# A fixed order, read from a table, for the vector, scalar and transfer work beside a matmul-bound token phase

## The chip, the cores and the metric

The kernel runs on one core of a Trainium2 chip. The core has TensorE (PE, matmuls; the profile lists its weight loads apart as PEld), VectorE (DVE), ScalarE (ACT), GpSimd (POOL) and SyncE (SP, which here only issues transfers). Each engine works through its own queue in order; semaphores tie the queues together. The metric is the device time of one execution in microseconds.

## The reference

The input x is (8, 3008, 256). Every sequence is Fourier-transformed along its 3008 rows, mixed by a complex 256x256 weight, shrunk towards zero by 0.01, and transformed back. The 24064 resulting rows ("tokens") go through a two-layer network with a squared relu.

```python
X = np.fft.rfft(x, axis=1)
Yr = Xr @ w_r - Xi @ w_i + b_r
Yi = Xr @ w_i + Xi @ w_r + b_i
Yr = np.sign(Yr) * np.maximum(np.abs(Yr) - lam, 0.0)      # Yi likewise
y = np.fft.irfft(Yr + 1j * Yi, n=3008, axis=1)
h = y.reshape(24064, 256) @ w_in                          # 256 -> 2048
r = np.maximum(h, 0.0)
out = (s * (r * r) + b) @ w_out                           # 2048 -> 256
```

## The kernel before

3008 = 94 x 32, and each transform is done by matmuls in steps: one over the 94 (`s1_units`, matmuls `x,A_t` into `u`), a pass through DRAM that regroups rows (`ud`, loaded as `us`), one over the 32 with the mixing and shrinking (`s23_units`: `fwd_unit` makes `xf`, `sum_unit` makes `s`, `mix_unit` and `shrink` work in the tile `ring`, `inv_unit` makes `v`), another pass through DRAM (`vd`, loaded as `vs`), and the last transform (`s4_units`) into `yt`, the token activations in 16 bits, transposed. `shrink` ends with the row swaps: 64-partition pieces of `ring` are moved to other partitions by transfers that SP issues (line 732), four for each of a sequence's first ten units. Sequence 1 shrinks unit by unit; the later ones take two units at once, and then issue eight transfers.

The first sequence is done alone, in the first 47 us (`first_batch`). After that comes the token phase: 48 tiles of up to 512 tokens. A tile takes 16 slots (`mc`). In each slot the first layer's matmuls for 128 of the 2048 hidden columns go to the double bank `psh`; every second slot ends with a relu of 1024 columns from `psh` to the f32 tile `rt` (line 879, on ACT) and a square into the 16-bit tile `gt` (line 889 on ACT or line 892 on DVE). In between run the previous tile's second layer, from `gt` and `w_out_t` into the banks `psa`, and pieces of the next sequence's transforms, through the two banks `psf`. Which piece goes into which slot is written in `plan`.

Some tiles use a scheme with seven products in place of eight for the second layer (`seven_mms`). It needs sums of blocks of `gt` (`s_op`, line 990 on DVE, tiles `s` and `gt`, and one accumulating transfer on POOL, line 983) and prepared sums of w_out (`T_s`). Its results leave PSUM through DVE adds at line 1023 into `zz` and `ost`. Where only the two `psa` banks serve, the fourth product (`psa<-T_s,s`) needs the bank that products one and two filled, so it waits for two adds: one into `zz`, one into `ost`. The results are stored from `ost` by SP (line 907 for most tiles).

The order of the engines' queues is set by the framework's scheduler, which works from its own estimates and from priorities; copies out of PSUM, relus and final adds are marked urgent (`urgent()`). Whether a copy or a square goes to DVE or ACT is decided when the code is recorded, by running sums of estimated work (`evac`, `act_first`, `work`); relus always go to ACT and final adds to DVE.

Of the kernel before, what the change touches and what calls it, by code (L numbers as in the profile page):

```python
# [9 lines left out]
F16 = mybir.dt.float16  # L10
# [9 lines left out]
VSCALE = 1.0 / 64.0  # L20

# [75 lines left out]
def kernel(  # L97
# [70 lines left out]
    lean = [0.0]  # L168

    pe = {"on": False, "now": 0.0}  # L170

    def matmul(out, lhs, rhs, **how):
        if pe["on"]:
            pe["now"] += 0.0025 + int(np.prod(rhs.shape[1:])) / 2400.0
        return nc.tensor.matmul(out, lhs, rhs, **how)  # L175

    def work(engine, us):
        load[engine] = max(load[engine], pe["now"]) + us

    def act_first(ready, ta, td):  # L180
        return max(load["act"], ready) + ta <= max(load["dve"], ready) + td + lean[0]

    def urgent():

        return tc.high_priority(offset=200) if pe["on"] else nullcontext()

    def evac(dst, src, cols):
        ta, td = over["act"] + cols / 1200.0, over["dve"] + cols / 960.0
        with urgent():
            if act_first(pe["now"], ta, td):  # L190
                work("act", ta)
                return None, nc.scalar.copy(out=dst, in_=src)  # L192
            work("dve", td)
            return nc.vector.tensor_copy(out=dst, in_=src), None
# [3 lines left out]
    def mix_bank():  # L198
        return pools["m"].tile([P, 512], F32, name="psm", tag="psm")
# [10 lines left out]
    def two_banks():  # L210
        return pools["h"].tile([P, 2, 512], F32, name="psh", tag="psh")

    def one_bank():
        return fpool.tile([P, 512], F32, name="psf", tag="psf")
# [4 lines left out]
    def other_bank():  # L219
        return apool.tile([P, 512], F32, name="psa", tag="psa")  # L220
# [6 lines left out]
    def emit_load_x(b, first=None, chunks=range(N2 // XCH)):  # L227
        xv = x[b].rearrange("(n1 n2) d -> n1 (n2 d)", n2=N2)
        for c in chunks:
# [4 lines left out]
            if first is not None:  # L234
                gate = nc.gpsimd.tensor_copy(out=t[0:1, 0:1], in_=first)
# [133 lines left out]
    last_square = [None]  # L369
# [4 lines left out]
    def make_t(i):  # L374

        if not T_s:
            nc.vector.tensor_tensor(
                out=b_21, in0=bias_bc[:, P:D], in1=bias_bc[:, 0:P], op=ALU.subtract
            )
            T_s.append(x2pool.tile([P, 4, MC // 2, P], F16, name="T_s", tag="x2"))  # L380
        t = T_s[0]
        a, b, op = (
            (w_block(0, 1), w_block(0, 0), ALU.subtract),
            (t[:, 0], w_block(1, 1), ALU.subtract),
            (w_block(1, 1), w_block(0, 1), ALU.subtract),
            (w_block(1, 0), t[:, 1], ALU.add),
        )[i]
        with tc.issue_after(last_square[0].ins):
            nc.vector.tensor_tensor(out=t[:, i], in0=a, in1=b, op=op)
        work("dve", 0.61)  # L390
# [9 lines left out]
    def make_bias():  # L400
# [3 lines left out]
        nc.scalar.activation(out=bias_bc, in_=ps[:, 0:D], func=AF.Copy, scale=bb_bc)  # L404
# [3 lines left out]
    ring = []  # L408
    yts = {}
    tails = {}  # L410
# [3 lines left out]
    def first_batch():  # L414
# [121 lines left out]

        def turn(ec, n):

            ps = mix_bank() if ec == 0 else any_bank() if n < HW else one_bank()
            for j in range(4):  # L540
# [5 lines left out]
            evac(  # L546
                vs[(0, h)][:, k : k + 4, ec * P : (ec + 1) * P],
# [5 lines left out]
        def last_dft(ec, n):  # L553
# [5 lines left out]
            else:  # L559
                ps = other_bank() if n % 8 else one_bank()  # L560
            for j in range(4):
# [6 lines left out]
            evac(  # L568
                yt[:, ec, n : n + 4, :],
                ps[:, 0:384].rearrange("p (j n) -> p j n", n=96), 384,  # L570
            )

# [51 lines left out]
    def s1_units(b, more_banks=False):  # L624

        ud = dpool.tile([96, N2, D], F16, name="ud", tag="ud")
        hold = {}

        def unit(i):
# [4 lines left out]
            ps = any_bank() if more_banks else one_bank()  # L634
            matmul(
# [4 lines left out]
            evac(u[0:96, k : k + 2, :], ps[0:96, :].rearrange("p (j d) -> p j d", j=2), 512)  # L640
            if k == UCH - 2:
                n = 2 * i + 2
                nc.sync.dma_start(out=ud[:, n - UCH : n, :], in_=u[0:96])

        def take_rows(which=range(4)):
            uv = ud.rearrange("k n d -> (k n) d").rearrange("(q p) d -> p q d", p=P)
            for q in which:
                t = uspool.tile([P, 6, D], F16, name="us", tag="us")
                nc.sync.dma_start(out=t, in_=uv[:, 6 * q : 6 * q + 6, :])
                us[(b, q)] = t  # L650
# [3 lines left out]
    def s23_units(b):  # L654
# [6 lines left out]
        hold = {}  # L661

        def fwd_unit(i):
# [3 lines left out]
            t = us[(b, i // 3)]  # L667
            for j in range(2):
# [7 lines left out]
            evac(xt[:, 1:3].rearrange("p r c k -> p (r c k)"), bank, 512)  # L676
            nc.vector.tensor_tensor(out=xt[:, 0], in0=xt[:, 1], in1=xt[:, 2], op=ALU.add)  # L677
            work("dve", 0.34)
            xf[i] = xt

        def sum_unit(h):

            ps = one_bank().rearrange("p (i e) -> p i e", i=2)
# [6 lines left out]
            s = mpool.tile([P, 2, D], F32, name="s", tag="m")  # L690
            with urgent():
                nc.scalar.copy(out=s, in_=ps)
            work("act", 0.49)
            hold[h] = s

        def mix_unit(i):
            ps = one_bank().rearrange("p (r e) -> p r e", r=2)
            xt = xf.pop(i)
            for r in range(2):
# [5 lines left out]
            with urgent():  # L705
                nc.vector.tensor_tensor(  # L706
                    out=ring[0][:, i % 4], in0=ps,
                    in1=hold[i // 2][:, i % 2].unsqueeze(1).to_broadcast([P, 2, D]), op=ALU.add,
                )
            work("dve", 0.67)  # L710
# [5 lines left out]
        def shrink(i, n):  # L716
# [4 lines left out]
            nc.vector.tensor_tensor(out=m, in0=t, in1=lo, op=ALU.max)  # L721
            nc.vector.tensor_tensor(out=m, in0=m, in1=hi, op=ALU.min)
            nc.vector.tensor_tensor(out=t, in0=t, in1=m, op=ALU.subtract)
            work("dve", 0.21 + 0.8 * n)
            for k in range(i, i + n):
                z = ring[0][:, 6 + k % 6]
                for j in range(2):
                    for r in range(2):
                        o = z[64 * r : 64 * r + 64, j]
                        a = t[64 * j : 64 * j + 64, k - i, r]  # L730
                        if k < H - 2:
                            nc.sync.dma_start(out=o, in_=a)
                        else:
                            nc.vector.tensor_copy(out=o, in_=a)
                            work("dve", 0.13)
                zt[k] = z

        def inv_unit(i):
            ps = one_bank().rearrange("p (j e) -> p j e", j=2)
            z = zt.pop(i)  # L740
            for j in range(2):
# [7 lines left out]
            evac(v[:, h : h + 2, :], ps, 512)  # L749
            if i % 2 == 1:  # L750
                nc.sync.dma_start(
                    out=vd[2 * i - 2 : 2 * i + 2].rearrange("q p e -> p q e"), in_=v
                )
            if i == H - 1:
                hold["vv"] = vd.rearrange("q (k n) e -> (q k) (n e)", n=N2)
# [4 lines left out]
        def take_half(h):  # L760
            t = vspool.tile([96, HW, D], F16, name="vs", tag="vs")
            nc.sync.dma_start(
                out=t.rearrange("k n e -> k (n e)"),
                in_=hold["vv"][:, h * HW * D : (h + 1) * HW * D],
            )
            vs[(b, h)] = t
# [17 lines left out]
    def s4_units(b):  # L784
# [6 lines left out]
        def unit(g):  # L791
# [4 lines left out]
            ps = one_bank()  # L796
            for j in range(w):
# [6 lines left out]
            evac(  # L804
                yt[:, ec, n2 : n2 + w, 0:N1],
                ps[:, 0 : w * N1].rearrange("p (j n) -> p j n", n=N1), w * N1,
            )
            if g == len(groups) - 1 and b >= 2:
# [3 lines left out]
                nc.gpsimd.tensor_copy(out=tails[pr][:, :, half], in_=yt[:, :, :, 80:94])  # L812
# [22 lines left out]
    hold_h = {}  # L835

# [21 lines left out]
    def first_mm(ti, mc):  # L858
# [4 lines left out]
        ps = hold_h["ps"]  # L863
        for dc in range(DC):
# [12 lines left out]
        rt = rpool.tile([P, 2, 512], F32, name="rt", tag="rt")  # L877
        with urgent():
            nc.scalar.activation(out=rt[:, :, 0:w], in_=ps[:, :, 0:w], func=AF.Relu)  # L879
# [4 lines left out]
        rr = rt[:, :, 0:w]  # L884
        if halves(ti):
            rr = rr.rearrange("p k (i t) -> p k i t", i=2)
        work("act", 0.07 + w / 600.0)
        if act_first(pe["now"], 0.09 + w / 600.0, 0.07 + w / 480.0):
            nc.scalar.activation(out=gt, in_=rr, func=AF.Square)  # L889
            work("act", 0.09 + w / 600.0)  # L890
        else:
            last_square[0] = nc.vector.tensor_tensor(out=gt, in0=rr, in1=rr, op=ALU.mult)  # L892
            work("dve", 0.07 + w / 480.0)
    def store(tl, sub, src):
        kind, b, j, w = tl
        if kind == "wide":
# [3 lines left out]
            nc.sync.dma_start(  # L900
                out=rows[n2 : n2 + 4, lo : lo + w], in_=src[0 : 4 * w]
            )
            return
        if kind == "main":
            rows = out[b * N + 512 * j : b * N + 512 * (j + 1), :]
            rows = rows.rearrange("(n1 n2) d -> n2 n1 d", n2=N2)[8 * sub : 8 * sub + 8]
            nc.sync.dma_start(out=rows, in_=src)
# [4 lines left out]
        while i < end:  # L912
# [14 lines left out]
            nc.sync.dma_start(out=dst, in_=src[i - i0 : i - i0 + cnt])  # L927
            i += cnt

    def second_mms(ti):  # L930
# [6 lines left out]
        def mm(sub, mc):  # L937
# [3 lines left out]
            if h == 0 and mc == 0:  # L941
                hold["ps"] = sum_bank(ti).rearrange("p (h e) -> p h e", h=2)
            ps = hold["ps"]
            matmul(
# [5 lines left out]
            if mc == MC - 1 and (alone or h == 1 or sub == nsub - 1):  # L950
                k = h + 1
                ost = opool.tile([P, 2, D], F32, name="ost", tag="ost")
                with urgent():
                    nc.vector.scalar_tensor_tensor(  # L954
                        out=ost[0:size, 0:k], in0=ps[0:size, 0:k], scalar=s_bc[0:size],
# [3 lines left out]
                work("dve", 0.13 + 0.27 * k)  # L959
                for i in range(k):  # L960
                    store(tl, sub - k + 1 + i, ost[:, i, :])
# [7 lines left out]
    sums = {}  # L969

# [4 lines left out]
    def s_op(ti, n, q):  # L975

        size = 2 * sub_size(tiles[ti])
        if n == 1:
# [213 lines left out]
```

## Time and profile before

| | |
|---|---|
| median of 3 runs | 836.48 us (836.18 to 836.76) |
| profiled execution | 837.46 us, its span 835.7 us |
| TensorE clock granted | 1.00 |
| busy: PE / DVE / ACT / POOL | 820.7 / 703.9 / 723.0 / 86.3 us |
| chain that ended last | PE 78%, DVE 9%, ACT 5%, DMA 5% |
| relu, 128x1024 on ACT (line 879) | 327 in the token phase, 1.03 us each |
| square, 128x1024 on DVE / ACT | 207 of 1.22 us / 121 of 1.06 us |
| `ring<-ring` transfers of 32 KB | 280 |

The duration of an instruction on DVE or ACT includes its end phase, beside which the next one already starts; two squares on DVE that wait for nothing start 1.14 us apart. The chain names, for each moment, the work that the end of the execution depended on. A wait row reads: engine and line that waited, what released it, total us, times, longest us.

### The profile page before, as it was taken

To read this page: it belongs to the slowest core of one execution; us is meant where nothing else is said; L and a number is where in the kernel's file an instruction comes from. 1 tells how busy PE (TensorE), PEld (TensorE's weight loads), DVE (VectorE), ACT (ScalarE), POOL (GpSimd) and SP (SyncE) were. 2 spreads that over 40 slices of the span, in tenths; PEclk is the share of its full clock that TensorE was granted. 3 is DMA by queue.
4 is the path that set the end of the run, shared out by engine and by line. 5 is a ranking of instruction groups with operands and counts; after the bars stand their busy time and mean duration, and the time that the engine had idled before them with its cause. 6 is when DMAs were issued, how large, how long until landed. Compare 5 with 4: busy or idle time off the path is not lost.

```text
span 835.7 us, 19552 instructions
## 1 busy us (share of the span) xinstructions
PE 820.7 (98%) x7662; PEld 598.5 (72%) x7662; DVE 703.9 (84%) x1104; ACT 723.0 (87%) x962; POOL 86.3 (10%) x114
## 2 busy tenths in 40 slices
PE   7999999999999999999999999999999999999997
PEld 6857767777677767777677776777767777767765
DVE  5988979978898888987889888797888988879785
ACT  5998988998899988998899988989879988788882
POOL 4550001100011001100011000100001000001000
PEclk9999999999999999999999999999999999999999
DMA  8954578346773378445773458724565233513321
GB/s 201 178 155 102 116 193 208 61 97 138 193 185 66 96 182 200 124 104 137 182 191 71 97 137 208 183 48 114 128 178 141 59 103 100 135 45 77 77 62 59
DMA packets 116670, 107.17 MB, mean 128 GB/s; under 512 B 12774, under 2 KB 100842, under 8 KB 115234
## 3 DMA queue, kind: packets, MB, share of 16 engines
q1 hardware_dynamic: 102498, 80.55, 34.0%
q0 software_dynamic: 14080, 25.37, 19.1%
q8 instruction: 60, 0.98, 0.5%
q14 instruction: 32, 0.26, 0.1%
HBM read 53.52 MB, written 46.66 MB: 120 GB/s over the span
## 4 chain that ended last, share of the span: by engine, by line
PE 78%; DVE 9%; ACT 5%; DMA 5%; issue 2%; POOL 0%; SPq 0%; DVEq 0%; POOLq 0%
PE psh L175 32%; PE psa L175 28%; PE psf L175 17%; ACT rt L879 2%; DVE gt L892 2%; DMA vd<-v 1%; DMA ring<-ring 1%; DMA x<-in_x_dram 1%; DVE ring L706 1%; DVE gt L990 1%; PE psm L175 1%; DVE ost L1023 1%; DMA vs<-vd 1%; ACT gt L889 1%; DVE s L990 1%
## 5 line engine op out<-in xcount | busy, mean ns | idle before, releaser
L879 ACT ACTIVATE rt<-psh 128x1024 f32<-128x1024 f32 (+2 forms) x384 | 386.9, 1009 | 56.0 <-PE psh L175 54.0
L175 PEld LDWEIGHTS <-gt 128*128 128x128 f16 (+1 forms) x3696 | 304.9, 101 | 167.2 <-issue 0.5
L175 PE MATMUL psh<-yt,w_in 128*128 128x512 f16 (+1 forms) x1344 | 396.7, 378 | 0.1
L892 DVE TENSOR_TENSOR gt<-rt 128x1024 f16<-128x1024 f32 (+2 forms) x239 | 286.0, 1201 | 81.3 <-ACT rt L879 80.6
L175 PE MATMUL psa<-w_out_t,gt 128*128 128x256 f16 (+3 forms) x2448 | 310.3, 253 | 0.0
L175 PEld LDWEIGHTS <-w_in 128*128 128x128 f16 x1536 | 136.5, 98 | 25.4 <-issue 2.9
L889 ACT ACTIVATE gt<-rt 128x1024 f16<-128x1024 f32 (+2 forms) x145 | 150.8, 1040 | 3.4
L175 PE MATMUL psa<-T_s,gt 128*128 128x128 f16 (+1 forms) x944 | 79.4, 219 | 0.0
L983 POOL DMA_DIRECT2D gt<-gt x42 | 38.0, 905 | 325.7 <-PE psh L175 87.3
L192 ACT CAST u<-psf 96x512 f16<-96x512 f32 x96 | 55.7, 582 | 9.1 <-PE psf L175 8.4
L706 DVE TENSOR_TENSOR ring<-psf,s 128x512 f16<-128x512 f32 x84 | 57.4, 684 | 4.1 <-PE psf L175 3.1
L192 ACT CAST v<-psf 128x512 f16<-128x512 f32 x79 | 45.8, 583 | 14.0 <-PE psf L175 13.5
L175 PE MATMUL psh<-tail,w_in 128*128 128x512 f16 (+1 forms) x192 | 52.1, 352 | 0.0
L239 POOL DMA_DIRECT2D x<-in_x_dram x36 | 19.2, 538 | 315.6 <-PE psf L175 314.4
L175 PEld LDWEIGHTS <-xf 128*128 128x128 f16 x504 | 46.7, 98 | 5.8 <-DVE xf L677 0.4
L175 PE MATMUL psf<-W_g,xf 128*128 128x256 f16 x336 | 50.4, 272 | 0.0
L192 ACT CAST yt<-psf 128x470 f16<-128x470 f32 (+2 forms) x84 | 43.1, 535 | 3.4 <-PE psf L175 2.2
L1023 DVE SCALAR_TENSOR_TENSOR ost<-psa,s_bc,zz 128x256 f32<-128x256 f32 (+1 forms) x80 | 34.7, 477 | 7.9 <-PE psa L175 6.4
L954 DVE SCALAR_TENSOR_TENSOR ost<-psa,s_bc,bias_bc 128x512 f32<-128x512 f32 (+2 forms) x51 | 37.1, 727 | 4.8 <-PE psa L175 2.6
L192 ACT CAST xf<-psf 128x512 f16<-128x512 f32 x64 | 37.5, 586 | 3.8 <-PE psf L175 3.7
L175 PE MATMUL psf<-x,A_t 94*96 94x512 f16 x102 | 39.0, 382 | 1.0 <-ACT yt L192 0.3
L175 PE MATMUL psf<-C_t,vs 96*128 96x94 f16 (+1 forms) x484 | 38.0, 205 | 0.1
(118 smaller groups left out, 797.0 us busy)
## 6 DMA issues: line engine op xcount, KB each, us to landing
out_dram<-ost SPq DMA_DIRECT2D x152, 128.0 KB
ud<-u SPq DMA_DIRECT2D x56, 192.0 KB
us<-ud SPq DMA_DIRECT2D x28, 384.0 KB
vd<-v SPq DMA_DIRECT2D x42, 256.0 KB
vs<-vd SPq DMA_DIRECT2D x14, 768.0 KB
x<-in_x_dram POOLq DMA_DIRECT2D x28, 376.0 KB, 6.3
gt<-gt POOLq DMA_DIRECT2D x38, 256.0 KB, 4.2
ring<-ring SPq DMA_DIRECT2D x280, 32.0 KB
```

The lines of the kernel that those rows point to most:

```text
L175: return nc.tensor.matmul(out, lhs, rhs, **how)
L192: return None, nc.scalar.copy(out=dst, in_=src)
L239: nc.gpsimd.dma_start(out=t[0:N1, i * w : (i + 1) * w], in_=xv[:, c * XCH * D + i * w : c * XCH * D + (i + 1) * w],)
L706: nc.vector.tensor_tensor(out=ring[0][:, i % 4], in0=ps, in1=hold[i // 2][:, i % 2].unsqueeze(1).to_broadcast([P, 2, D]), op=ALU.add,)
L879: nc.scalar.activation(out=rt[:, :, 0:w], in_=ps[:, :, 0:w], func=AF.Relu)
L889: nc.scalar.activation(out=gt, in_=rr, func=AF.Square)
L892: last_square[0] = nc.vector.tensor_tensor(out=gt, in0=rr, in1=rr, op=ALU.mult)
L954: nc.vector.scalar_tensor_tensor(out=ost[0:size, 0:k], in0=ps[0:size, 0:k], scalar=s_bc[0:size], in1=bias_bc[0:size].unsqueeze(1).to_broad ...
L983: nc.gpsimd.dma_start(out=a12, in_=a11, accum_op=ALU.add)
L990: nc.vector.tensor_tensor(out=out, in0=a, in1=b, op=op)
L1023: nc.vector.scalar_tensor_tensor(out=out, in0=of, scalar=s_bc[0:size], in1=other, op0=ALU.mult, op1=ALU.add)
```

## The change

All work of the token phase on ACT, DVE, SP and POOL is recorded as pieces (`later`), each with what it needs and the engines that could do it. A table `TURNS` holds two characters in base 36 for each piece; their number gives the piece's engine (remainder by 4: act, dve, sp, pool) and how many pieces later than its place of recording it is emitted. `pump`, called at each matmul, emits the pieces whose turn has come, and the framework is told to keep the order in which things are emitted (`manual_schedule`, all five engines). So engine and order of 2,525 pieces are fixed by the table, relus may also go to DVE, and the running sums decide only in the first batch.

In `shrink` the swaps of two units are one transfer of 64 partitions x 2 x 256 in place of two: four transfers instead of eight for a pair. `rt` and `ost` become three fixed buffers each. The loads of x lose two of three gate copies, and the fourth chunk of a sequence's x is recorded at slot 44 or 48 of the sequence instead of 54. PE's order is the same but for the first tiles of the token phase, where first-layer matmuls stand before some `x,A_t` matmuls, and a few exchanged neighbours.

```diff
+TURNS = (
+    "25253y20241x21251w26241s24242e1p2h3m363m2q1d20181c1k1x1o1h20213g1g1x251w30232j231s1g1s1t3o1s"
...
     def matmul(out, lhs, rhs, **how):
-        if pe["on"]:
-            pe["now"] += 0.0025 + int(np.prod(rhs.shape[1:])) / 2400.0
+        pump()
         return nc.tensor.matmul(out, lhs, rhs, **how)
...
+    def plan_turns():
+        at = [divmod(int(TURNS[k : k + 2], 36), 4) for k in range(0, len(TURNS), 2)]
+        queue.extend(
+            (k, ("act", "dve", "sp", "pool")[at[k][1]])
+            for k in sorted(range(len(at)), key=lambda k: k + at[k][0])
+        )
+
+    def begin(op, engine):
+        assert engine in op.cost and all(n.gone for n in op.needs)
+        op.gone = True
+        op.emit(engine)
+
+    def pump():
+        while queue and queue[0][0] < len(pieces):
+            k, engine = queue.pop(0)
+            begin(pieces[k], engine)
...
+    def later(emit, cost, needs=(), frees=None):
+
+        op = SimpleNamespace(emit=emit, cost=cost, needs=list(needs), gone=False)
+        if frees is not None:
+            reads[id(frees)].append(op)
+        if pe["on"]:
+            pieces.append(op)
+            return op
...
+    def leave_bank(dst, bank, src, cols, needs=()):
+        def emit(e):
+            (nc.scalar.copy if e == "act" else nc.vector.tensor_copy)(out=dst, in_=src)
+
+        return later(emit, copy_cost(cols), needs=needs, frees=bank)
...
+            moves = []
+            for j in range(2):
+                for r in range(2):
+                    o = ring[0][64 * r : 64 * r + 64, z0 : z0 + n, j]
+                    a = t[64 * j : 64 * j + 64, :, r]
+                    if i + n <= H - 2:
+                        moves.append(later(
+                            lambda e, o=o, a=a: nc.sync.dma_start(out=o, in_=a),
+                            {"sp": 0.6 + 0.05 * n}, needs=[done],
+                        ))
+                        continue
...
-                        if k < H - 2:
-                            nc.sync.dma_start(out=o, in_=a)
-                        else:
-                            nc.vector.tensor_copy(out=o, in_=a)
-                            work("dve", 0.13)
...
+        def relu(e):
+            if e == "act":
+                nc.scalar.activation(out=rt, in_=ps[:, :, 0:w], func=AF.Relu)
+            else:
+                nc.vector.tensor_scalar(
+                    out=rt, in0=ps[:, :, 0:w], scalar1=0.0, scalar2=None, op0=ALU.max
+                )
...
+        first = later(
+            relu, {"act": 0.065 + w / 600.0, "dve": 0.065 + w / 480.0},
+            needs=squares[-len(rts) :][:1] if len(squares) >= len(rts) else [], frees=ps,
+        )
+        squares.append(later(
+            square, {"act": 0.1 + w / 600.0, "dve": 0.065 + w / 480.0}, needs=[first]
+        ))
...
-            nc.sync.dma_start(out=rows, in_=src)
+            send(rows.rearrange("(n1 n2) d -> n2 n1 d", n2=N2)[8 * sub : 8 * sub + 8], src)
...
+                a = add(base, 0, 0.39, needs=left_ops[-3:])
+                b = add(top, 1, 0.39, needs=[a, *new_o(0)])
...
+    plan_turns()
+    osts = [opool.tile([P, 2, D], F32, name="ost", tag="ost") for _ in range(3)]
+    rts = [rpool.tile([P, 2, 512], F32, name="rt", tag="rt") for _ in range(3)]
+    ctx.enter_context(tc.manual_schedule(engines={
+        mybir.EngineType.PE, mybir.EngineType.Activation, mybir.EngineType.DVE,
+        mybir.EngineType.SP, mybir.EngineType.Pool,
+    }))
...
-            for c, at in enumerate((10, 14, 26, 54)):
+            free_at = 37 + 4 * (mark[b] - s1 - 50) // 16
+            for c, at in enumerate((10, 14, 26, free_at)):
```

## The prediction

> **What bounds the kernel now.** I read the page first: the busy line, then the chain that ended last.
>
> ```profile
> PE 820.7 (98%) x7662; PEld 598.5 (72%) x7662; DVE 703.9 (84%) x1104; ACT 723.0 (87%) x962; POOL 86.3 (10%) x114
> ...
> PE 78%; DVE 9%; ACT 5%; DMA 5%; issue 2%; POOL 0%; SPq 0%; DVEq 0%; POOLq 0%
> ```
>
> TensorE (PE) sets the time; DVE and ACT are nearly full beside it and own 14% of the chain. A busy PE row hides small waits, because the end of a matmul is modelled: in the timeline a 128-column matmul is shown as 0.22 us, yet seven in a row start 0.055 us apart. So I took PE's spacing from start to start, against the median spacing of its shape (0.056 us for 128 columns, 0.109 for 256, 0.216 for 512). All matmuls at those medians make 806.6 us. What lies above them is 9.8 us before 46 us (the first batch, which the change leaves alone) and 13.7 us after. The latter is all that an order of the other engines can win. It splits into: 5.0 us in 9 places where `psa<-T_s,s` waits; 2.6 us in 16 places where a matmul into `psf` waits for a copy or sum of DVE or ACT; 1.7 us in 6 places at transfers (1.0 of it one wait at 111.8 us); 0.8 us in 4 places at the start of the token phase; 0.5 us at `psh` and at the end; and 3.1 us in pieces below 0.06 us, which I leave where they are.
>
> Next the waits. The largest is one pattern:
>
> ```profile
> PEld L175 <- DVE ost L1023: 5.1, 9, 0.9
> ...
> PE psf L175 <- DMA ring<-ring: 0.9, 1, 0.9
> ```
>
> The timeline of DVE at one of the nine, and PE's row that it released:
>
> ```profile
> 456.75 0.68 DVE L706 TENSOR_TENSOR ring<-psf,s 128x512 f16<-128x512 f32 x1
> 457.35 1.22 DVE L892 TENSOR_TENSOR gt<-rt 128x1024 f16<-128x1024 f32 x1
> 458.49 0.68 DVE L721 TENSOR_TENSOR ring<-ring,low 128x1024 f16<-128x1024 f16 x1
> 459.09 0.68 DVE L990 TENSOR_TENSOR gt<-gt 128x1024 f16<-128x1024 f16 x1
> 459.69 0.48 DVE L1023 SCALAR_TENSOR_TENSOR zz<-psa,s_bc,bias_bc 128x256 f32<-128x256 f32 x1
> 460.08 0.68 DVE L722 TENSOR_TENSOR ring<-ring,high 128x1024 f16<-128x1024 f16 x1
> 460.68 0.48 DVE L1023 SCALAR_TENSOR_TENSOR ost<-psa,s_bc,zz 128x256 f32<-128x256 f32 x1
> ...
> 460.07 0.50 PE L175 MATMUL psa<-T_s,gt 128*128 128x128 f16 x6
> 461.22 0.23 PE L175 MATMUL psa<-T_s,s 128*128 128x128 f16 x1 [0.65 <-DVE ost L1023]
> ```
>
> The two adds at L1023 empty the `psa` bank that PE wants. The last of the six matmuls starts at 460.07 + 5 x 0.0555; the next was due at 460.40 and came 0.81 us late. DVE never paused: a square (1.14), a `ring` step (0.60) and a `gt` sum (0.60) stand ahead of the adds, another `ring` step (0.60) between them. That is a matter of order. Last, the end:
>
> ```profile
> 829.65 0.48 DVE L954 SCALAR_TENSOR_TENSOR ost<-psa,s_bc,bias_bc 128x256 f32<-128x256 f32 x1 [0.56 <-PE psa L175]
> 831.40 0.48 DVE L954 SCALAR_TENSOR_TENSOR ost<-psf,s_bc,bias_bc 128x256 f32<-128x256 f32 x1 [1.26 <-PE psf L175]
> ...
> 829.12 3.40 SPq L907 DMA_DIRECT2D out_dram<-ost  x4
> ```
>
> SP sends three stores while PE still works; one store is left behind the last add, and the span ends 3.8 us after that add.
>
> **The change part by part.** The sum is made against the profiled execution: 837.46 us, of which the span is 835.7; the median of the runs is 0.98 below it.
>
> *Order on DVE around the adds.* Seventeen tiles before the last batch use this scheme with only two `psa` banks. As built, 13 of them had one DVE instruction between the two adds, now none has. At the place above, DVE now does the `ring` sum and three 16-bit sums (4 x 0.60) and then the two adds; the square has gone to ACT. From the same 456.75 the adds end at 456.75 + 2.40 + 0.39 + 0.48 = 460.02, before 460.40. The other seventeen places leave 0.9 to 1.6 us by the same kind of sum. Of 5.0 us I take 4.7 as gone. What is late next is the 3.1 us of small pieces. Bounds: nothing gone (0) to 5.0.
>
> *Copies, relus and squares dealt out anew.* Counts as built: on DVE 62 relus more (none before), 104 squares fewer, 116 copies out of PSUM more; ACT the reverse. Intervals from start to start when nothing waits: square 1.138 DVE, 0.965 ACT; copy of 512 columns 0.60 DVE, 0.48 ACT; relu 0.93 ACT. A relu on DVE isn't in the trace: between 1.138 (the square, as many f32 elements) and 1.20 (two copies); I take 1.14, one instruction being nearest to the square. DVE: 62 x 1.14 - 104 x 1.138 + 116 x 0.60 = +22 us; ACT: -58 + 100 - 56 = -14 us. Beside PE's 807 us both stay under 90%, so the work itself is hidden. If the cover failed everywhere, it would cost those 22 us on the path. [...]
>
> Does the new order serve PE's other waits? For each result of DVE or ACT that PE waits for after 60 us I set the intervals queued on its engine against PE's own spacing from release to need: 14 come out late in the old order, 2 (by 0.05 and less) in the new, and the rest have 0.3 us or more. Waits of DVE on ACT or transfers aren't in that sum, and it misses most of the 0.81 above, so I take 2.0 of the 2.6 us, not all. Bounds: -1 (new waits for a blocked queue) to 2.6.
>
> *Row swaps.* 280 transfers of 32 KB become 40 of 32 KB and 120 of 64 KB; 120 issues fewer. Eight issues take 5.6 us in the timeline of SP, so SP saves some 78 us; PE sees that only where a swap comes too late. The first of a pair is complete after four issues as before (2.8 us), the second 2.8 us sooner; each transfer carries twice the bytes. A swap lands 1.3 us after its issue by median, 6.5 at worst; a 256 KB `vd` write, the larger neighbour, 3.1. So 0 to 1.8 us more; I take little over 0. [...]
>
> But the fixed order on SP puts stores into the swaps of the second sequence (b = 1, not merged): the last swap of unit 9 now stands behind two stores. From there to PE's need I count 4.0 us less DVE's own lag of about 1, formerly 6.8. Landings at 100 to 110 us have a median of 4.8 and a worst of 6.3, so I expect 1.8 us of wait there and 0.5 elsewhere early (at 68 and 72 us of PE time 3.6 to 3.9 are left): 2.5 us of transfer waits in place of 1.7, a loss of 0.8. Bounds: a gain of 1.2 to a loss of 3.3.
>
> *POOL* issues one gate copy instead of three and asks for the fourth chunk of x some 6 to 10 slots earlier. It waited 314 us for PE before those loads; without that cover, a chunk takes 6.3 us to land and is wanted over 25 us later. Nothing.
>
> *Start of the token phase.* PE's order now has w_in matmuls where `x,A_t` matmuls stood. The first needs a copy of `yt` which DVE, backlogged there, delivers 2.5 us late by the queue's sum; the worst was 2.1. Loss 0.4; bounds 0 to 1.5.
>
> *The end.* As built, SP holds two earlier stores until after the last one. Issue spacing 0.65 us: the span's end moves by 2 x 0.65 = 1.3 us. Nothing hides that. Bounds 0.6 to 1.3.
>
> Sum: -4.7 - 2.0 + 0.8 + 0.4 + 1.3 = -4.2 us. 837.46 - 4.2 = 833.3 for a profiled execution, 836.48 - 4.2 = **832.3** for the median.
>
> **The rivals.**
> Nearly clean: swaps land in time and all 16 `psf` waits go too: -5.0 - 2.6 - 1.2 + 0.4 + 1.3 = -7.1, so 829.4, or 828 with a start that costs nothing and half of the small pieces. For it: the margins of the queue sums; against: landings of up to 6.5 us.
>
> No gain: DVE, 22 us fuller, reaches the adds as late as before, because what it waits for (ACT's relus: 80.6 us of waiting before L892) now blocks it in a fixed order. The 4.7 stay: 837.0. Against it: all seventeen places have the square moved away or margin.
>
> Slower: the fixed queue of SP as the new limit. Every sequence ends its swaps close ahead of PE's need; a swap behind a store that waits for DVE delays all seven. One us at each makes 832.3 + 7 = 839. It decides from 0.6 us each. For it: SP waited 78.9 us for L1023 adds at L907, with up to 13.1 in one piece. Against: 120 issues fewer, and margins of 5 us and more after b = 1.
>
> **How the numbers follow.** A run of this kernel tells from no change about 0.2%, 1.7 us: faster is below 834.8, slower above 838.2. Chances: the forecast 0.60 (its own range 830.3 to 834.7), nearly clean 0.18, no gain 0.11, slower 0.11. Range 828 to 837: it leaves out the slower case and little below. Faster 0.78, same 0.11, slower 0.11.
>
> **What would show it.** Waits of PE's weight loads for L1023's successor under 1 us in all, and the two adds side by side in DVE's timeline; relus on DVE of 1.14 us spacing; three stores on SP after the last add and 5 us from that add to the span's end; a `ring` wait near 110 us. The forecast is wrong if PE waits in new places behind SP or behind a DVE that stands still for ACT.

## The result and the profile after

The change made the kernel slower: 845.54 us (844.55 to 846.66, four runs) against 836.62 us (836.18 to 837.41), a ratio of 1.0106 with an interval of 1.0088 to 1.0123. I had forecast 832.3 us and a range that ends at 837. The profiled execution took 845.85 us, its span 844.1 us; before, the span was 835.7.

The page of the changed kernel, its busy line and its chain:

```profile
PE 821.6 (97%) x7662; PEld 601.3 (71%) x7662; DVE 729.1 (86%) x1178; ACT 705.8 (84%) x888; POOL 84.5 (10%) x112
...
PE 77%; DMA 11%; DVE 7%; ACT 3%; issue 1%; SPq 1%; POOL 0%; DVEq 0%; ACTq 0%; POOLq 0%
```

The share of DVE in the chain fell from 9% to 7%, that of the transfers rose from 5% to 11%: the end of the execution now depends on transfers for some 50 us more than before. PE's waits (and DVE's, where it waits for a transfer) say which transfers:

```profile
DVE ring L891 <- DMA ring<-ring: 4.6, 4, 2.6
...
PEld L235 <- DMA gt<-gt: 2.9, 3, 1.1
PE psf L235 <- DMA ring<-ring: 2.7, 4, 1.2
PEld L235 <- DMA vs<-vd: 2.6, 3, 1.5
PE psa L235 <- DMA gt<-gt: 2.4, 3, 0.9
PE psf L235 <- DMA vs<-vd: 2.1, 3, 1.3
PE psf L235 <- DVE xf L298: 1.5, 1, 1.5
PEld L235 <- DMA us<-ud: 1.0, 1, 1.0
```

A weight load and the matmul behind it often wait for the same transfer (`vs` above, 2.6 and 2.1 us in three waits each), so such rows aren't added. Every kind of transfer is there: swaps, both passes through DRAM (`us<-ud`, `vs<-vd`) and the accumulating `gt` transfers. The row that was the largest before, PE's weight loads behind the `ost` adds with 5.1 us, is gone. At the place that the prediction used, DVE and PE now show:

```profile
464.93 0.68 DVE L1268 TENSOR_TENSOR gt<-gt 128x1024 f16<-128x1024 f16 x1
465.53 0.68 DVE L1268 TENSOR_TENSOR s<-gt 128x1024 f16<-128x1024 f16 x1
466.25 0.69 DVE L1268 TENSOR_TENSOR gt<-gt 128x1024 f16<-128x1024 f16 x1
466.86 0.48 DVE L1325 SCALAR_TENSOR_TENSOR zz<-psa,s_bc,bias_bc 128x256 f32<-128x256 f32 x1
467.37 0.48 DVE L1325 SCALAR_TENSOR_TENSOR ost<-psa,s_bc,zz 128x256 f32<-128x256 f32 x1
...
468.33 0.44 PE L235 MATMUL psa<-T_s,gt 128*128 128x128 f16 x5
468.61 0.22 PE L235 MATMUL psa<-T_s,s 128*128 128x128 f16 x1
```

The two adds stand side by side behind three sums, as counted, and `psa<-T_s,s` follows 468.33 + 5 x 0.0555 without a wait. The end of the execution:

```profile
836.39 0.48 DVE L1225 SCALAR_TENSOR_TENSOR ost<-psa,s_bc,bias_bc 128x256 f32<-128x256 f32 x1 [1.00 <-PE psa L235]
838.14 0.48 DVE L1225 SCALAR_TENSOR_TENSOR ost<-psf,s_bc,bias_bc 128x256 f32<-128x256 f32 x1 [1.26 <-PE psf L235]
...
835.42 5.14 SPq L1162 DMA_DIRECT2D out_dram<-ost  x4
```

From the end of the last add (838.62) to the end of the span there are now 5.5 us, 3.8 before.

Measured as in the prediction (PE's spacing from start to start above the median of its shape), the 8.4 us of span come from these places, in us, each rounded by itself:

| | forecast | measured | before -> after |
|---|---|---|---|
| `psa<-T_s,s` behind the adds | -4.7 | -4.9 | 5.0 -> 0.1 |
| `psf` behind copies and sums | -2.0 | +1.3 | 2.6 -> 3.9 |
| transfers | +0.8 | **+9.2** | 1.7 in 6 places -> 10.9 in 14 |
| start of the token phase | +0.4 | +1.1 | 0.8 -> 1.9 |
| last matmul to the end of the span | +1.3 | +1.7 | 4.6 -> 6.3 |
| first batch, before 46 us | 0 | +0.8 | 9.8 -> 10.6 |
| all else, pieces below 0.06 us among it | 0 | -0.6 | |

One row carries the result. It is mostly not the speed of the transfers. From the traces I took, for each transfer, its landing time (end of the issue to landing) and its lead (end of the issue to the first matmul that reads it, with any wait of that matmul inside):

| us | landing, median: before | after | lead, smallest / median: before | after |
|---|---|---|---|---|
| `ring<-ring` | 1.3 | 1.8 | 3.8 / 9.2 | 1.9 / 7.3 |
| `vs<-vd` | 7.2 | 6.2 | 7.3 / 10.2 | 5.5 / 8.5 |
| `us<-ud` | 5.0 | 4.5 | 4.2 / 22.4 | 5.3 / 15.8 |
| `gt<-gt` | 3.5 | 3.9 | 3.8 / 7.4 | 4.1 / 6.2 |

By median, swaps and `gt` transfers land half a us later and the two passes half a us to one us sooner. The leads fell by 1.2 to 6.6 us by median, and for swaps and `vs` in the smallest too. PE waits where a lead would be shorter than the landing. Two things can make an issue late: what stands ahead of it on SP, and data that DVE finishes later. Both had changed. From the end of the second unit's mix to the end of the subtraction, a shrink of two units on DVE took 3.2 us before and 4.1 after, by median; and writes to `vd` whose data is ready stood on SP for 2.8 us in the median and 10.4 at most, 0.03 and 6.5 before.

### The profile page after: what moved, and what is told of

Its sections match the earlier page's. It is cut to its first block, busy times and chain, and to the rows that moved or that the text cites. A ratio compares the mean times of both kernels' runs of the same rounds, so it can differ in the third digit from the quotient of the medians.

```text
span 844.1 us, 19222 instructions
## 1 busy us (share of the span) xinstructions
PE 821.6 (97%) x7662; PEld 601.3 (71%) x7662; DVE 729.1 (86%) x1178; ACT 705.8 (84%) x888; POOL 84.5 (10%) x112
## 4 chain that ended last, share of the span: by engine, by line
PE 77%; DMA 11%; DVE 7%; ACT 3%; issue 1%; SPq 1%; POOL 0%; DVEq 0%; ACTq 0%; POOLq 0%
PE psh L235 31%; PE psa L235 28%; PE psf L235 16%; DMA ring<-ring 3%; DMA vs<-vd 3%; DMA gt<-gt 2%; DMA vd<-v 2%; PE psm L235 1%; DVE gt L1138 1%; ACT rt L1125 1%; ACT gt L1136 1%; DVE ring L891 1%; DMA x<-in_x_dram 1%; DVE rt L1127 1%; DMA us<-ud 1%
## 5 line engine op out<-in xcount | busy, mean ns | idle before, releaser
L1125 ACT ACTIVATE rt<-psh 128x1024 f32<-128x1024 f32 (+2 forms) x322 | 323.8, 1007 | 72.7 <-PE psh L235 67.6
L1136 ACT ACTIVATE gt<-rt 128x1024 f16<-128x1024 f32 (+2 forms) x249 | 256.0, 1042 | 6.6 <-DVE rt L1127 4.5
L1138 DVE TENSOR_TENSOR gt<-rt 128x1024 f16<-128x1024 f32 (+2 forms) x135 | 161.2, 1202 | 5.7 <-ACT rt L1125 5.1
L1127 DVE TENSOR_SCALAR rt<-psh 128x1024 f32<-128x1024 f32 (+1 forms) x62 | 74.1, 1197 | 21.3 <-PE psh L235 14.9
L891 DVE TENSOR_TENSOR ring<-psf,s 128x512 f16<-128x512 f32 x84 | 57.6, 686 | 21.4 <-PE psf L235 15.8
L298 DVE CAST u<-psf 96x512 f16<-96x512 f32 x53 | 36.0, 680 | 8.7 <-PE psf L235 8.5
L298 ACT CAST xf<-psf 128x512 f16<-128x512 f32 x59 | 34.1, 583 | 8.9 <-PE psf L235 8.8
L298 ACT CAST yt<-psf 128x470 f16<-128x470 f32 (+2 forms) x70 | 35.7, 519 | 4.2 <-PE psf L235 2.9
L298 ACT CAST v<-psf 128x512 f16<-128x512 f32 x43 | 25.0, 583 | 14.2 <-PE psf L235 14.2
```

The lines of the kernel that those rows point to most:

```text
L298: (nc.scalar.copy if e == "act" else nc.vector.tensor_copy)(out=dst, in_=src)
L891: lambda e: nc.vector.tensor_tensor(out=ring[0][:, i % 4], in0=ps, in1=hold[i // 2][:, i % 2].unsqueeze(1).to_broadcast([P, 2, D]), op=ALU ...
L1125: nc.scalar.activation(out=rt, in_=ps[:, :, 0:w], func=AF.Relu)
L1127: nc.vector.tensor_scalar(out=rt, in0=ps[:, :, 0:w], scalar1=0.0, scalar2=None, op0=ALU.max)
```

## The experiments

Theories at the start: A, transfers are issued too shortly ahead of need by the fixed order; B, the merged swaps are the loss; C, transfers land more slowly. PE's lost time in each profile, after 46 us, and the end, in us:

| kernel | time | ratio to before | PE lost | at transfers | `psf` | `T_s` | end |
|---|---|---|---|---|---|---|---|
| before | 836.6 | | 13.7 | 1.7 | 2.6 | 5.0 | 4.6 |
| changed | 845.5 | 1.0106 | 19.7 | 10.9 | 3.9 | 0.1 | 6.3 |
| SP, POOL left to the scheduler | 835.9 | 0.9975 | 14.0 | 7.2 | 2.0 | 0.1 | 4.6 |
| SP alone left to the scheduler | 841.1 | 1.0044 | 16.4 | 8.6 | 3.7 | 0.1 | 4.6 |
| swaps and passes ahead on SP | 837.5 | 0.9998 | 11.6 | 2.9 | 3.7 | 0.1 | 6.1 |
| swaps alone ahead | 841.6 | 1.0047 | 15.9 | 8.5 | 3.4 | 0.1 | 6.5 |
| passes alone ahead | 843.2 | 1.0078 | 17.5 | 7.1 | 4.1 | 0.1 | 6.4 |
| both, end and `tail` edited | 836.6 | 0.9993 | 12.5 | 3.3 | 2.9 | 0.1 | 4.6 |
| shrink earlier on DVE | 853.7 | 1.0197 | 26.4 | 6.6 | 14.0 | 1.3 | 6.1 |
| shrink, sums earlier; SP, POOL free | 854.4 | 1.0205 | 30.2 | 3.6 | 13.1 | 5.5 | 4.6 |
| eight transfers for a pair | 850.2 | 1.0160 | 23.6 | 15.2 | 4.6 | 0.1 | 6.3 |
| eight, swaps and passes ahead | 842.2 | 1.0063 | 15.9 | 8.2 | 3.7 | 0.1 | 6.1 |
| before, with merged swaps | 838.8 | 1.0019 | 14.0 | 1.5 | 2.6 | 5.2 | 5.3 |
| small stores | 838.7 | 1.0019 | 14.1 | 5.8 | 4.3 | 0.1 | 4.3 |

Each ratio is to runs of the kernel before made beside that kernel, on the same chip; beside the experiments their medians were 836.97 to 837.27 us.

**SP and POOL out of the fixed order.**

```diff
     ctx.enter_context(tc.manual_schedule(engines={
         mybir.EngineType.PE, mybir.EngineType.Activation, mybir.EngineType.DVE,
-        mybir.EngineType.SP, mybir.EngineType.Pool,
     }))
```

> The changed kernel, but SP and POOL are left out of the fixed order: the table still fixes PE, ACT and DVE, the scheduler again orders the transfers. Theory A (transfers are issued too shortly ahead of PE's need, by the fixed order of SP's queue and by the later shrink on DVE): the writes to vd and ud no longer stand behind swaps and stores that wait for DVE, and the stores at the end go out in the order in which they are ready. Of the 10.9 us that PE loses at transfers the part behind SP's queue goes, about 3 to 5, and about 1.5 at the end: 839 to 841.5 us; the rest stays, because the shrink is still late on DVE. Theory B (the merged swaps, of twice the bytes, are themselves the loss): 843 to 845, only the end gains. Theory C (transfers land more slowly because more of them meet): 843 to 846. If all of it were SP's queue: 835 to 837.

It took 835.9 us, a ratio of 0.9975 (0.9958 to 0.9992): all of the loss is gone, and this kernel is a little faster than the one before. By the time that is the last case of the expectation. The profile bears it out only in part: it is of the slowest of ten runs (838.06 us), and 7.2 us at transfers are still there, among them 3.8 of weight loads behind `gt` transfers. The end is 4.6 us again.

**The swaps split again, and merged in the kernel before.**

```diff
-                            lambda e, o=o, a=a: nc.sync.dma_start(out=o, in_=a),
...
+                            for rr in range(2):
+                                nc.sync.dma_start(
+                                    out=ring[0][64 * rr : 64 * rr + 64, z0 + j, r],
+                                    in_=t[64 * r : 64 * r + 64, j, rr],
+                                )
```

> The changed kernel, but each swap of two units is two transfers of one unit again (the first two pieces carry the first unit of the pair, the last two the second), at the same places of the table. Theory B (the merger is the loss): the first unit is complete sooner and each transfer is half as large, so most of the 10.9 us at transfers goes: 836 to 840 us. Theory A: the transfers are late for other reasons, and 120 more issues of some 0.6 us delay what stands behind them on SP: 845 to 850. Theory C: about 845, the bytes are the same.

850.19 us, ratio 1.016 (1.0129 to 1.0191), at the upper end of the case of A. PE's and DVE's waits at swaps grow:

```profile
DVE ring L891 <- DMA ring<-ring: 7.1, 8, 1.5
PEld L235 <- DMA ring<-ring: 5.4, 6, 1.5
PE psf L235 <- DMA ring<-ring: 5.0, 6, 1.3
```

```diff
+            if n == 2 and i + n <= H - 2:
+                z0 = 6 + i % 6
+                for j in range(2):
+                    for r in range(2):
+                        nc.sync.dma_start(
+                            out=ring[0][64 * r : 64 * r + 64, z0 : z0 + n, j],
+                            in_=t[64 * j : 64 * j + 64, :, r],
+                        )
...
```

> The kernel before with one part of the change alone: the swaps of two units are four transfers instead of eight; order and engines are left to the scheduler and the running sums. Theory B: PE loses some 5 us or more at the swaps, 840 to 844 us. Theory A and C: the merger by itself costs at most some tenths of a us at single places and frees SP of 120 issues: 835.5 to 838.

838.83 us, ratio 1.0019 (1.0004 to 1.0034), a little above the expectation of A. Its profile has no loss at swaps (transfers 1.5 us); the end is 0.7 longer. Theory B is out from both sides: the merger helps the changed kernel by some 4.5 us (1.0106 against 1.0160) and hardly touches the old one.

**Small stores.**

```diff
+            if kind == "main":
+                dst, part = dst[0:1], part[0:16]
             outs[number].append(later(
```

> The changed kernel, but each store of a main tile carries only its first 16 partitions, an eighth of the bytes; the rest of the output is not written. Number and order of the issues stay. Theory C (landings are slow because stores, swaps and passes meet): the landings of vs and ring get shorter by 1 us or more and PE's wait at transfers falls from 10.9 to some 4 us: 837 to 840 us. Theory A (issued too late): the landing of a pass of 256 KB is its own length, only the worst places gain: 842 to 845.

This kernel leaves most of the output unwritten. 838.66 us, ratio 1.0019 (1.0002 to 1.0036), inside the range of C. The median leads are those of the changed kernel within 0.5 us, the landings shorter by 0.3 to 0.8 us (1.5, 5.4, 4.0, 3.3 in the order of the table above). That was worth 5.1 of the 10.9 us at transfers, and 1.9 at the end, where the last stores are small too. So PE's waits are the difference of two quantities that lie close together, and half a us of either counts. As the main cause of the change's loss C is out all the same: from before to after the two passes land sooner. The swaps and `gt` transfers do land 0.5 and 0.4 us later, and what that adds to their waits wasn't measured apart; but with swaps and passes ahead on SP, below, most of the waits at swaps go although a swap still lands in 1.7 us by median. My expectation was wrong to price A as if only the worst places could gain.

**Which engine's order.** Theories D: SP's order alone; E: POOL's has a part; F: DVE's later shrink has a part.

```diff
-        mybir.EngineType.SP, mybir.EngineType.Pool,
+        mybir.EngineType.Pool,
```

> The changed kernel, but SP alone is left out of the fixed order; POOL keeps it. Theory D (SP's queue order is what the change lost on; POOL's order does nothing): the same as with both left out, 835 to 838 us, last matmul to end 4.6 us. Theory E (POOL's fixed order, which issues the accumulating gt transfers and the loads of x, held part of the loss): 839 to 843.

841.05 us, ratio 1.0044 (1.0029 to 1.0059): E by the time. In the profile the waits at swaps and passes are nearly gone, and the `gt` transfers, which POOL issues, are the worst of all kernels:

```profile
PEld L235 <- DMA gt<-gt: 8.1, 8, 2.1
PE psa L235 <- DMA gt<-gt: 6.7, 8, 1.9
```

They aren't issued later than with POOL free (median lead 6.4 us against 6.2), but five of the 42 take 7.1 us or more to land, against 5.9. The two kernels differ in POOL's order alone: SP, DVE and ACT work through the same sequences. So POOL's fixed order costs those 5 us (1.0044 against 0.9975). In the profiles, whose spans differ by 2.9 us, 1.7 of it is the wait at `psf` behind the long square of the last section. Why the `gt` transfers land later isn't settled.

**SP in fixed order, but swaps and passes ahead of stores.** A piece marked `early` is emitted up to 10 places of the table sooner, once it and its needs are there.

```diff
     def pump():
-        while queue and queue[0][0] < len(pieces):
-            k, engine = queue.pop(0)
-            begin(pieces[k], engine)
+        while queue:
+            for w in sorted(w for w in ahead if w[0] - EARLY <= queue[0][0]):
+                if all(n.gone for n in pieces[w[1]].needs):
+                    ahead.remove(w)
+                    if not pieces[w[1]].gone:
+                        begin(pieces[w[1]], w[2])
...
-                            {"sp": 0.6 + 0.05 * n}, needs=[done],
+                            {"sp": 0.6 + 0.05 * n}, needs=[done], early=True,
...
-            v_writes.append(later(write, {"sp": 0.5}, needs=v_ops[-2:]))
+            v_writes.append(later(write, {"sp": 0.5}, needs=v_ops[-2:], early=True))
...
-            half_loads[(b, h)] = later(load_half, {"sp": 0.45}, needs=v_writes)
+            half_loads[(b, h)] = later(load_half, {"sp": 0.45}, needs=v_writes, early=True)
...
```

> The changed kernel with all five engines in the fixed order, but on SP the swaps, the writes and the loads of the passes through DRAM (ud, us, vd, vs) are emitted as soon as they and what they need are recorded, up to 10 places of the table earlier, so in front of stores that formerly stood ahead of them; no other engine's order moves. Theory D: the transfers of the transform no longer stand behind stores that wait for DVE, PE's wait at transfers falls from 10.9 to some 6 or 7 us, and the end keeps its 6.25: 839 to 842 us. If it is not the stores ahead of them: 844 to 847, or more, when SP now waits at a swap and holds back stores.

837.47 us, ratio 0.9998 (0.9985 to 1.0012): better than D had it. No engine but SP changed its order, and 8.0 us of PE's waits at transfers went. Most of the 2.9 that are left is one wait at a `gt` transfer. Its chain, and its largest rows at transfers of the token phase:

```profile
PE 88%; DVE 5%; DMA 3%; ACT 1%; issue 1%; POOL 0%; SPq 0%; DVEq 0%; ACTq 0%; POOLq 0%
...
PEld L235 <- DMA gt<-gt: 2.0, 1, 2.0
PE psa L235 <- DMA gt<-gt: 1.8, 1, 1.8
DVE ring L906 <- DMA ring<-ring: 1.0, 1, 1.0
PEld L235 <- DMA ring<-ring: 0.4, 1, 0.4
```

This is the mechanism at one place, the load of `vs` for which PE waited 1.5 us at 234.8 us of the changed kernel. SP's timeline there, and PE's row:

```profile
220.93 0.62 SPq L1162 DMA_DIRECT2D out_dram<-ost  x1
221.65 0.42 SPq L966 DMA_DIRECT2D vd<-v  x1
222.12 0.62 SPq L1162 DMA_DIRECT2D out_dram<-ost  x1
222.92 0.81 SPq L798 DMA_DIRECT2D ud<-u  x1
223.81 0.61 SPq L966 DMA_DIRECT2D vd<-v  x1
224.47 1.49 SPq L798 DMA_DIRECT2D ud<-u  x1
228.90 0.32 SPq L982 DMA_DIRECT2D vs<-vd  x1
...
234.80 0.38 PE L235 MATMUL psf<-C_t,vs 96*128 96x94 f16 x5 [1.31 <-DMA vs<-vd]
```

and DVE's, from the same profile:

```profile
220.15 0.75 DVE L1225 SCALAR_TENSOR_TENSOR ost<-psa,s_bc,bias_bc 120x512 f32<-120x512 f32 x1
221.07 1.23 DVE L1127 TENSOR_SCALAR rt<-psh 128x1024 f32<-128x1024 f32 x1 [0.17 <-PE psh L235]
222.21 0.68 DVE L298 CAST u<-psf 96x512 f16<-96x512 f32 x1
```

The data of the first `vd<-v`, from two copies, was ready at 217.82, when DVE's ended. It stood 3.8 us behind a store whose add ended at 220.90. The second was ready at 220.67 and stood 3.1 us behind a write of `u` whose copy on DVE ended at 222.89. The load of `vs` can start only when these writes have landed (the last at 228.82), and it landed at 234.75. SP's timeline of the same stretch with passes ahead of stores, where PE runs 3.0 us sooner:

```profile
214.86 3.16 SPq L981 DMA_DIRECT2D vd<-v  x2
218.07 0.49 SPq L813 DMA_DIRECT2D ud<-u  x1
218.66 1.32 SPq L1177 DMA_DIRECT2D out_dram<-ost  x2
221.02 0.33 SPq L997 DMA_DIRECT2D vs<-vd  x1
...
230.29 0.37 PE L235 MATMUL psf<-C_t,vs 96*128 96x94 f16 x5
```

The second write's data is ready at 217.63, the same point of PE's work (220.67 less 3.0), and leaves at once, as does the first. The load starts 7.9 us sooner, 4.8 by PE's work, lands at 227.29, and PE comes for it at 230.29 without a wait. In this place DVE was as late as before; only what stood ahead on SP had changed.

**The two halves of that edit,** the swaps alone and the writes and loads alone (the same diff with only those marks):

> Of the run that took swaps and passes ahead of stores on SP (span 835.3 us against 844.1), only the part of the swaps: they are emitted up to 10 places of the table earlier, the writes and loads of ud and vd stay where the table has them. The waits at swaps of the changed kernel's profile (ring 5.6 us) and at the passes (vs 2.6, us 0.9) are the shares to tell apart. If a swap's place in the queue is what counts, because everything else follows from it: 838 to 840 us. If both count by their waits: 840 to 842.5, with the waits at vs and us left.

841.64 us, 1.0047 (1.0032 to 1.0063).

> The other part alone: the writes to ud and vd and the loads of us and vs up to 10 places earlier, the swaps as the table has them. If both count by their waits: the 3.5 us at vs and us go, the swaps' 5.6 stay: 840.5 to 843 us. If the swaps alone count: 844 to 846.

843.24 us, 1.0078 (1.0061 to 1.0094). The first lies in the range for "both count by their waits", the second 0.2 us above it. PE's lost time is 3.8 and 2.2 us less; together the halves remove 8.1, which is 2 more than the sum, though by the times such a difference is within the intervals. The rows suggest where it comes from. Each half removes its own kind's waits for the most part: with swaps alone DVE's row at swaps falls from 4.6 to 1.3 us, while PE's `psf` row at `vs` stays near its 2.1 (1.8); with passes alone the rows at `vs` and `us` are gone, but PE's `psf` row at swaps grows from 2.7 to 4.7. So the passes moved ahead on SP's one queue seem to have held up the swaps; by how much a swap was issued later wasn't measured.

**The eight transfers under the better order.**

> Swaps and passes ahead of stores on SP, and each swap of two units in two transfers again, eight for a pair. In the changed kernel's own order the split cost 4.7 us. If the merger matters only where SP's queue is late: 837 to 839, near the 837.5 of the same order with merged swaps. If it is worth as much in any order: 841 to 843.

842.21 us, 1.0063 (1.0049 to 1.0077), against 837.47 merged. The case of 837 to 839 fell: here the merger is worth about 5 us in either order (4.5 and 5.4 by the ratios, which the intervals don't tell apart). The smallest lead of a swap is 3.8 us merged and 2.4 split. So the split lost in both orders: 850.2 against 845.5 us in the table's, 842.2 against 837.5 in this one.

**The shrink earlier on DVE** (`early` on its three steps, SP as the table has it):

```diff
-                cost, needs=[one],
+                cost, needs=[one], early=True,
-                cost, needs=[two],
+                cost, needs=[two], early=True,
...
```

> The changed kernel with all five engines in the fixed order, but the three steps of each shrink on DVE are emitted up to 10 places of the table earlier (some 3 us); relus, squares and copies move back behind them, SP's order stays. Theory F (DVE's later shrink, 4.4 us from mix to subtraction instead of 3.1, is a second part of the loss): swaps are ready 1 to 2 us sooner, SP's queue moves on sooner, PE's waits at swaps (5 us) shrink to 1 or 2: 838 to 842 us. Theory D alone: swaps that are ready sooner still wait for their place on SP, 843 to 846.

853.68 us, ratio 1.0197 (1.0174 to 1.022), above both cases of the expectation. The shrink did get earlier, 2.2 us from mix to subtraction in place of 4.1 (counted as above, not as in the expectation), and PE's waits at transfers fell from 10.9 to 6.6 us. But what moved back behind it on DVE came late, above all the small sums of `xf`:

```profile
PEld L235 <- DVE xf L866: 6.9, 12, 1.3
PE psf L235 <- DVE xf L866: 3.8, 8, 1.0
```

In the changed kernel the first of these rows (there L851) had 0.8 us. The same with SP and POOL free and the `gt` sums earlier too:

> SP and POOL left out of the fixed order, and on DVE the steps of the shrink and the sums of gt up to 8 places of the table earlier. In the run with SP and POOL left out, PE still waited 7.2 us for transfers, 3.7 of it for the accumulating gt transfers and 2.2 for swaps. Theory F: some 4 of these 7.2 go: 831 to 834 us. Without a part of DVE in the loss: 835 to 838, with new waits for relus and copies that were moved back it may be slower.

854.39 us, 1.0205 (1.0188 to 1.0223), again above both cases: waits at transfers are halved against the run with SP and POOL free (3.6 for 7.2), `psf` and `T_s` pay 16.5 for it. That agrees with F, by which swaps that are ready sooner are waited for less, but doesn't show it: in both runs PE also stood longer at other places (26.4 and 30.2 us lost in all), which gives every transfer more time. As a remedy F is useless: the table's order on DVE trades the shrink's lag for the adds and sums. With swaps and passes ahead the same lag of 4.1 us cost little.

**The end, and a square of 3.15 us.** Two edits on top of the better order on SP: `early` for the stores of the last two tiles, and the copies to `tail` on ACT.

```diff
-                    lambda e: nc.gpsimd.tensor_copy(
+                    lambda e: nc.scalar.copy(
                         out=tails[pr][:, :, half], in_=yt[:, :, :, 80:94]
...
-                lambda e: nc.sync.dma_start(out=dst, in_=part), {"sp": 0.65}, needs=[op]
+                lambda e: nc.sync.dma_start(out=dst, in_=part), {"sp": 0.65}, needs=[op],
+                early=tl in tiles[-2:],
```

> Swaps and passes ahead of stores on SP (span 835.3 us), and two more edits: the stores of the last two tiles go out in the order in which their adds are recorded, and the six copies of yt to tail, on POOL before, are done by ACT. The end should fall from 6.1 to 4.6 us. A square on DVE took 3.15 us instead of 1.22 in the one place where it ran beside such a copy on POOL (2 us late, PE waits 1.68): if the two engines hinder each other there, that wait goes; if it has another cause, it stays. Together 835.3 - 1.5 - 1.7 = 832.1 us of span, 833 to 835 in time; 834.5 to 836.5 if the wait of 1.68 stays.

836.58 us, ratio 0.9993 (0.9979 to 1.0007), no difference to the kernel before, and just above both cases of the expectation; the span is 834.6. The end is 4.6 us again, and the wait of 1.68 us at `psf<-F_t,us` is gone. Of the 3.2 us won so, 2.5 came back as new small waits, for `zz`, `gt`, `xf` and at two transfers; ACT is 4.5 us fuller, and whether that is their cause wasn't tried.

## Why the prediction was wrong

**The step that failed** is the paragraph on row swaps: "2.5 us of transfer waits in place of 1.7, a loss of 0.8. Bounds: a gain of 1.2 to a loss of 3.3." It was 10.9 us in place of 1.7. I summed SP's queue for the swaps, found one narrow place at b = 1, and took the landing of a swap as 1.3 us, but for 4.8 at that place. Three things were missing. The passes and the `gt` transfers weren't in the sum at all, though each of the two passes is a write, its landing, a load and its landing in a row; `vs<-vd` had a lead of 7.3 us in its worst case against a landing of 7.2 in the median, which the trace of before would have shown. But for about 1 us of lag at b = 1, a transfer's data was taken as ready when SP came to it, while SP in fact stood still for DVE at a store and had ready writes behind it (those to `vd` stood 2.8 us in the median). And bounds built from one place's margin stood for all 244 transfers that PE reads. Moving swaps and passes ahead on SP alone took 8.0 of the 10.9 us away. The rest is for the most part at `gt` transfers, which POOL issues: the weight loads waited 2.9 us for them in the changed kernel and showed no such wait before. Which step of the change made these waits stays open.

**The rival that came closest** was "the fixed queue of SP as the new limit", given 0.11 and 839 us. Its mechanism is the one shown, a transfer behind a store that waits for DVE, though it named swaps alone and not the passes. Its price was set at seven places of 1 us; it was 14 places with a mean of 0.78, three of them at `gt` transfers. My ground against it, "margins of 5 us and more after b = 1", held for swaps in a sum without DVE's lag.

**Right:** the order around the adds (4.7 forecast, 4.9 measured, in every run that kept the table on DVE untouched), the end (1.3, measured 1.7, three stores after the last add as read from the order), relus on DVE at 1.14 us from start to start (262.62 to 263.76 in the timeline), and busy times of DVE and ACT of +25 and -17 us for a forecast of +22 and -14.

**Off in size:** the wait at b = 1 was to be 1.8 us and was 1.0, at 115.6 us. The start cost 1.1 us for 0.4 (0.94 at the first w_in matmul, behind a copy of `yt`, inside the bounds). The copies and sums for `psf` were to give 2.0 and cost 1.3; 1.68 of that is the long square below, without which they would have gained 0.4. The 0.8 us before 46 us is hardly the table's: with merged swaps alone, which come only later, the same stretch loses 10.5, and with the table and passes ahead 10.0.

With this better order on SP, the change would still not have brought 4.2 us. With passes ahead, the span is 835.3 against 835.7: -4.9 at the adds, +1.2 transfers, +1.1 `psf`, +1.1 start, +1.5 end, and some tenths.

## What to carry to other kernels

When the order of a transfer queue changes, list for every transfer its lead and its landing from the trace of before, and look for the smallest difference; the kinds with a chain of write, landing, load and landing come first (here `vs<-vd`, with 7.3 us of lead for 7.2 of landing). In a queue that works in order, put what waits for a busy engine and nobody needs soon (stores) behind what is ready and needed (swaps and passes: 8.0 of 10.9 us of PE's waits went); fixing the order of compute engines doesn't require fixing the transfers' (845.5 us with both fixed, 835.9 with SP and POOL free). A gain on one queue (4.9 us at the adds) can be real and still be less than what the same table loses on another (9.2 at transfers).

## What I hadn't expected of the hardware

A square on DVE that takes 1.22 us elsewhere took 3.15 us beside a copy on POOL, which itself took 1.58 in place of 0.93, and beside the issues of two x loads behind that copy. From the changed kernel, DVE and then POOL:

```profile
450.28 3.15 DVE L1138 TENSOR_TENSOR gt<-rt 128x1024 f16<-128x1024 f32 x1
453.35 0.68 DVE L298 CAST xf<-psf 128x512 f16<-128x512 f32 x1
...
450.76 1.58 POOL L1037 COPY tail<-yt 128x896 f16<-128x896 f16 x1
451.63 1.75 POOL L354 DMA_DIRECT2D x<-in_x_dram  x2
```

PE stood 1.68 us for the `xf` copy behind it. With the copy on ACT, the same square:

```profile
443.64 1.22 DVE L1153 TENSOR_TENSOR gt<-rt 128x1024 f16<-128x1024 f32 x1
444.78 0.68 DVE L313 CAST xf<-psf 128x512 f16<-128x512 f32 x1
```

Three other overlaps of a square and such a copy look different. In the changed kernel squares of 768 columns that began first, at 543.30 and 739.74, kept their 0.95 us, and the copies that began behind them took 1.41 and 1.48 in place of 0.93. With SP and POOL free the copy began 0.39 us before the square and took 1.27; the square took 1.95 in place of 1.22 and ended 1.07 us after it. In these three it is the one that began second that grew the most, by 0.48, 0.55 and 0.73 us.

The square above is the other way round: it began first, and yet it grew by 1.93 us and outlasted the copy by 1.09. In the run with shrink and sums earlier and SP and POOL free, the copy also began after the square (by 0.20 us), but no x issue stood behind it: the square took 1.21 us and the copy 1.80. So the extra length goes with the two x issues, which end 0.05 us before the square, as far as POOL's rough rows tell. The issues alone weren't varied, and no run shows by what the engines hinder each other.
